# One row in 48 of an output projection's weights loaded in four small transfers, and an announced empty loop at the end of VectorE's list

## The chip, the core and the metric

The kernel runs on one core of one Trainium2 chip. The metric is the device time of one execution in microseconds (us). Before the change three runs took 186.94, 187.01 and 187.04 us, median 187.01.

## What is computed

One decode step of a transformer block with adaptive layer norm, for two sequences of one token each. Cut to what matters:

```
mod = (silu(c) @ w_mod)            -> sa, ca, ga, sb, cb, gb     # 6 vectors of 640 per sequence
h = layernorm(x) * (1 + ca) + sa
q = h @ wq                         # 640 -> 32 heads of 192
k, v = k_cache, v_cache            # the last 1024 positions of each head
o = softmax(q k^T / sqrt(192)) v   # per sequence and head
x = x + ga * (o @ wo)              # 6144 -> 640
h = layernorm(x) * (1 + cb) + sb
x = x + gb * ((gelu(h @ w_gate) * (h @ w_up)) @ w_down)    # 640 -> 1536 -> 640
```

Everything is bfloat16 in memory. 76.88 MB are read in all, most of it the two caches; wo is 6144 x 640, 7.86 MB.

## The kernel before

The five engines each get a list of operations, written in program order by a small scheduler (`_Sched`): `S.op` puts an operation on an engine's list, `S.dma` a transfer on SyncE's (SP's) list, and `emit` (L133) writes each list out with the semaphore waits that reads and writes of named buffers require. There is no planner: an engine runs its list in order, and a wait at the head of a list holds back all that stands behind it. All transfers are issued by SP, so their order on SP's list is the order in which data comes.

A large SBUF buffer `store` holds all the streamed data: four ring slots of 64 cache rows per partition (24576 B each), and a region of 61440 B per partition behind them that first holds wq, then two more k or v pieces, then wo. The work runs so:

1. GpSimd and VectorE build constants; w_mod, c, x, wq and the first k piece are issued.
2. TensorE (PE) computes the modulation (L468), then q (L491), which is spread to all partitions as `qbc`.
3. Scores: for 8 k tiles in two halves, VectorE multiplies a half tile by q (L529), PE adds up over the 192 dimensions with an identity matrix (L548, in a loop over tiles), VectorE reduces the rest (L562).
4. Softmax for both sequences (L566 to L586).
5. Weighted sum: for each of 2 x 4 v tiles VectorE masks the weights per head (`d_mask`, L590) and PE multiplies (`p_pv`, L602). These are called PV(b,t) here.
6. The result is normalized (L615, L619), gathered per head (L627) and copied to `oc` (L672), on which VectorE runs three 32 x 32 block transposes (L675) to give `oT`: 48 pieces `oT[:, t, :]`, piece t holding the rows 48p + t of the 6144-long vector on partition p.
7. wo: row 48p + t of wo stands on partition p, so each partition reads 48 consecutive rows. They come in four transfers of 16, 16, 12 and 4 rows per partition (wo0 to wo3, L681). PE multiplies them as they land (L706), 4 matmuls per t, one for each of four groups of 160 output columns.
8. Second layer norm, w_gate (wg), w_up (wu) and w_down (wd0, wd1, wd2: 6, 4 and 2 of 12 rows per partition; L747), the residual, and the output transfer.

`warm` (L517) are PE matmuls whose result nobody reads. Two waits on SP's list matter for the change: wo0 to wo3 wait for PV(0,2) and PV(0,3), whose v tiles lay where wo goes (L682); wg and all behind it wait for PV(1,0) and PV(1,1) (L685). Slot 2 of the ring holds the v tile of PV(1,2), slot 3 that of PV(1,3).

Of the kernel before, what the change touches and what calls it, by code (L numbers as in the profile page):

```python
# [1 line left out]

# [2 lines left out]

ALU = mybir.AluOpType
ACTF = mybir.ActivationFunctionType
AX = mybir.AxisListType
BF16 = mybir.dt.bfloat16
F32 = mybir.dt.float32  # L10

_COMPUTE = ("pe", "dve", "act", "pool")

# [58 lines left out]
class _Sched:  # L72
# [57 lines left out]
                need[key] = (d.sem, d.val)  # L130
        return need

    def emit(self, engname, eng, tail=None):  # L133
        waited = {}
        cnt = 0

        def await_all(need):
            for key, (s, v) in need.items():
                if waited.get(key, 0) >= v:
                    continue  # L140
                eng.wait_ge(s, v)
                waited[key] = v

        done = None
        for o in self.lists[engname]:
            if o.loop is not None:
                if o.loop is done:
                    continue
                done = o.loop
                n, ahead, rounds = done.waits(self, engname)  # L150
                await_all(ahead)
                with eng.Fori(0, n) as i:
                    for r in range(done.period):
                        for key, (s, base, step) in rounds[r].items():
                            eng.wait_ge(s, i * step + base)
                        done.body(eng, i, r).then_inc(done.ops[r].sem, 1)
                for r in range(done.period):
                    for key, (s, base, step) in rounds[r].items():
                        waited[key] = max(waited.get(key, 0), base + step * (n - 1))
                cnt += len(done.ops)  # L160
                assert cnt == done.ops[-1].val
                continue
            await_all(self.needs(o, engname))
            last = o.fn(eng)
            if o.inc == 1:
                cnt += 1
                assert cnt == o.val, (engname, o.name, cnt, o.val)
            last.then_inc(o.sem, o.inc)
        if tail is not None:
            tail(eng)  # L170


def bass_adaLN_cond__sliding_block_cached__geglu_ffn__decode_kernel(
# [16 lines left out]
    B, _, D = A_x.shape  # L190
# [4 lines left out]
    SQ = 32  # L195
    NJ = P // SQ
# [4 lines left out]
    DN = D // NJ  # L201
# [9 lines left out]
    NT = NQ // P  # L211
# [3 lines left out]
    NQC = RN // QC  # L215
# [8 lines left out]
    SL = J * Dh  # L224
    WQ_SPLIT = [5]
    assert sum(WQ_SPLIT) == KT
    WO_SPLIT = [16, 16, 12, 4]
    OT_SPLIT = [16, 16, 16]
    assert sum(WO_SPLIT) == NT and sum(OT_SPLIT) == NT
    WU_SPLIT = [5]  # L230
    assert sum(WU_SPLIT) == KT
    WD_SPLIT = [6, 4, 2]
# [8 lines left out]
    with es:  # L241
        S = _Sched(nc, es)
        sb = lambda name, shape, dt: es.enter_context(nc.sbuf_tensor(name, shape, dt))
# [9 lines left out]
        def aux_f(a, n):  # L253
            assert a + n <= NAUX
            return aux[:, a:a + n]
# [8 lines left out]
        def tile_f(slot, n=1):  # L264
            return store[:, slot * SL:(slot + n) * SL]
# [7 lines left out]
        oc = aux_f(0, RN)  # L273
# [4 lines left out]
        ident_b = sb("ident_b", [P, P], BF16)  # L278
        ident_f = sb("ident_f", [P, P], F32)
        one = sb("one", [1, 1], F32)  # L280
        G32 = sb("G32", [P, SQ], F32)
        M32 = sb("M32", [P, H], F32)
        M32b = sb("M32b", [P, H], BF16)
        Bsel = sb("Bsel", [P, P], F32)
        SEL = sb("SEL", [P, 2, HM, P], BF16)
        DS = sb("DS", [P, P], F32)
        xc = sb("xc", [P, DN], BF16)
# [20 lines left out]
        gx = sb("gx", [1, H, QP], F32)  # L308
        nb = sb("nb", [P, 1], F32)
        E_sb = sb("E_sb", [P, 2, KP], BF16)  # L310
        Em = sb("Em", [P, 2, J, H], BF16)
        esum = sb("esum", [P, 2], F32)
        rden = sb("rden", [P, 2], F32)
        On = sb("On", [P, 2, Dh], BF16)
        ps = es.enter_context(nc.psum_tensor("ps", [P, 8, 512], F32))
# [7 lines left out]
        BK_M = 0  # L323
        SC = 256

        def bank(k):
            return ("bank", k)
# [4 lines left out]
        sem_wq = [S.sem("d_wq%d" % i) for i in range(len(WQ_SPLIT))]  # L332
        sem_wo = [S.sem("d_wo%d" % i) for i in range(len(WO_SPLIT))]
        sem_wg = S.sem("d_wg")
        sem_wu = [S.sem("d_wu%d" % i) for i in range(len(WU_SPLIT))]
        sem_wd = [S.sem("d_wd%d" % i) for i in range(len(WD_SPLIT))]
        sem_ring = [S.sem("d_ring%d" % i) for i in range(4)]
# [2 lines left out]
        def k_dma(dst, src):  # L340
            return lambda e: e.dma_start(dst, src)  # L341
# [5 lines left out]
        def dram_rows(v):  # L347
# [9 lines left out]
             reads=[("S", 0, 0, 0), ("S", 0, 0, 1), ("S", 0, 1, 0), ("S", 0, 1, 1)], writes=["ident_f"], name="ident_f")  # L357
        S.op("pool", lambda e: e.tensor_copy(out=ident_b[:, :], in_=ident_f[:, :]),
             reads=["ident_f"], writes=["ident_b"], name="ident_b")
# [3 lines left out]
             reads=["ident_f"], writes=["G32"], name="G32")  # L363
        S.op("dve", lambda e: e.tensor_reduce(out=M32[:, :], in_=ident_f[:, :].rearrange("p (h t) -> p h t", t=QP), axis=AX.X, op=ALU.add),
             reads=["ident_f"], writes=["M32"], name="M32")
# [3 lines left out]
             reads=["G32"], writes=["Bsel"], name="Bsel")  # L369
# [3 lines left out]
             reads=["M32"], writes=["DS"], name="DS")  # L373


        for b in range(2):
            S.op("dve", (lambda b: lambda e: e.tensor_copy(
                out=SEL[:, b, :, BS * b:P:SQ], in_=G32[:, :].rearrange("p (j m) -> p m j", m=HM)))(b),
                reads=["G32"], writes=["SEL"], name="SEL%d" % b)
        for b in range(2):  # L380
            for m in range(HM):
# [3 lines left out]
                    reads=["ident_f"], writes=["Qsel"], name="Qsel%d%d" % (b, m))  # L385
# [7 lines left out]
        keep = {}  # L393
# [14 lines left out]
        def slot_of(*it):  # L408
            return place[it]
# [87 lines left out]
        def move(eng, dst, src, reads, writes, name):  # L497
            if eng == "act":
                S.op("act", lambda e: e.activation(out=dst, in_=src, func=ACTF.Copy), reads=reads, writes=writes, name=name)
            else:  # L500
                S.op("dve", lambda e: e.tensor_copy(out=dst, in_=src), reads=reads, writes=writes, name=name)  # L501
# [15 lines left out]
        def warm(n, bk):  # L517
            def f(e):
                last = None
                for _ in range(n):  # L520
                    last = e.matmul(ps[:, bk, 0:2 * Dh], lhsT=ident_b[:, :], rhs=qbc[:, :, :].rearrange("p b d -> p (b d)"),  # L521
                                    start=True, stop=True)
                return last
            if n:
                S.op("pe", f, reads=["ident_b", "qbc"], writes=[bank(bk)], name="warm")
# [144 lines left out]
        assert keep["kv"] == len(items)  # L670
        for c in range(NQC):
            move(("act", "dve")[c % 2], oc[:, QC * c:QC * (c + 1)], ps[:, BK_H + c, 0:QC], [bank(BK_H + c)], [("oc", c)], "oc%d" % c)  # L672
        t0 = 0
        for i, nt in enumerate(OT_SPLIT):
            S.op("dve", (lambda t0, nt: lambda e: e.transpose(oT[:, t0:t0 + nt, :], oc.rearrange("p (q k) -> p k q", k=NT)[:, t0:t0 + nt, :]))(t0, nt),  # L675
                 reads=[("oc", c) for c in range(NQC)], writes=[("oT", t) for t in range(t0, t0 + nt)], name="oT%d" % i)
            t0 += nt

        wo_src = A_wo.rearrange("(p t) n -> p t n", t=NT)
        wo_of = [(sum(WO_SPLIT[:i]), sum(WO_SPLIT[:i + 1])) for i in range(len(WO_SPLIT))]  # L680
        for i, (ta, tb) in enumerate(wo_of):  # L681
            S.dma("sp", k_dma(wo_v[:, ta:tb, :].rearrange("p t n -> p (t n)"), wo_src[:, ta:tb, :].rearrange("p t n -> p (t n)")),  # L682
                  sem_wo[i], writes=[("wo", i)], deps=[keep["pv", 0, t] for t in (NTL - 2, NTL - 1)], name="ld_wo%d" % i)
        assert slot_of("v", 1, 0) == 0 and slot_of("v", 1, 1) == 1
        r3_dead = [keep["pv", 1, 0], keep["pv", 1, 1]]  # L685
        S.dma("sp", k_dma(wg_v.rearrange("p k n -> p (k n)"), B_w_gate.rearrange("(p k) n -> p (k n)", k=KT)), sem_wg,
              writes=["wg"], deps=r3_dead, name="ld_wg")
# [13 lines left out]
        for i, (ta, tb) in enumerate(wo_of):  # L701
            def f(e, ta=ta, tb=tb):
                last = None
                for t in range(ta, tb):
                    for j in range(NJ):
                        last = e.matmul(ps[SQ * j:SQ * j + SQ, BK_M, 0:DN], lhsT=oT[:, t, :], rhs=wo_v[:, t, DN * j:DN * j + DN],  # L706
                                        start=(t == 0), stop=(t == NT - 1), tile_position=(0, SQ * j), skip_group_check=True)
                return last
            S.op("pe", f, reads=[("wo", i)] + [("oT", t) for t in range(ta, tb)], writes=[bank(BK_M)], name="wo%d" % i)
            warm(WO_WARM[i], 1)  # L710

        S.op("dve", lambda e: e.tensor_tensor(out=lnt[:, 0, :], in0=ps[:, BK_M, 0:DN], in1=modC[:, 2, :], op=ALU.mult),  # L712
             reads=[bank(BK_M), ("modC", 0)], writes=[("lnt", 0)], name="ga_attn")
        S.op("dve", lambda e: e.tensor_tensor(out=X2[:, 0, :], in0=lnt[:, 0, :], in1=X2[:, 0, :], op=ALU.add),
             reads=[("lnt", 0)], writes=[("X2", 0)], name="x1")
# [3 lines left out]
        def ffn_gu(bk, wv, key, name, ka, kb):  # L719
            def f(e):  # L720
# [11 lines left out]
             reads=[bank(BK_G[0])], writes=["gl"], name="gelu")  # L732
        k0 = 0
        for ci, nk in enumerate(WU_SPLIT):
# [4 lines left out]
             reads=[bank(BK_G[1]), "gl"], writes=["aC"], name="geglu")  # L739
        to_contraction(aT[:, :, :], aC[:, :], FT, ["aC"], ["aT"], "aT")  # L740
        f0 = 0
        for ci, nf in enumerate(WD_SPLIT):
            def f(e, f0=f0, nf=nf):
# [11 lines left out]
             reads=[bank(BK_C), ("modC", 1)], writes=[("lnt", 1)], name="gb_y")  # L755
        S.op("dve", lambda e: e.tensor_tensor(out=sc[:, :], in0=lnt[:, 1, :], in1=X2[:, 0, :], op=ALU.add),
             reads=[("lnt", 1), ("X2", 0)], writes=["sc"], name="outC")
# [3 lines left out]
        nc.sync.wait_ge(sem_out, 16)  # L761
        S.emit("pool", nc.gpsimd)
        S.emit("act", nc.scalar)
        S.emit("dve", nc.vector)
        S.emit("pe", nc.tensor)


# [26 lines left out]
```

## Time and profile before

| | |
|---|---|
| runs, median (lowest to highest) | 187.01 us (186.94 to 187.04) |
| profiled execution: its own time | 187.73 us |
| profiled execution: span from first to last instruction | 186.5 us (186.47) |
| PE busy | 117.4 us, 63% |
| VectorE (DVE) busy | 106.6 us, 57% |
| ScalarE (ACT) busy | 13.9 us, 7% |
| GpSimd (POOL) busy | 4.9 us, 3% |
| read from HBM | 76.88 MB, 412 GB/s over the span |
| data queue (q1) | 2916 packets, 96.4% of 16 engines' span |

How to read what the prediction shows. The page cuts the span into 40 slices of 4.66 us; in the DMA row each digit is the busy share of the 16 DMA engines in tenths, and the row below is what they moved. The queue list gives packets, MB and the share of the engines' time. The chain of waits lists start (us), length (us) and what ran; "SPq" is SP issuing a transfer. In the timeline a line is start, length, engine, source line, operation, output<-inputs, count, and in brackets the idle time before and what ended it. "Landing" is when a transfer's last semaphore count arrives. The trace also records each DMA packet (queue, start, duration, size), though not which of the 16 engines moved it.

### The profile page before, as it was taken

To read this page: it belongs to the slowest core of one execution; us is meant where nothing else is said; L and a number is where in the kernel's file an instruction comes from. 1 tells how busy PE (TensorE), PEld (TensorE's weight loads), DVE (VectorE), ACT (ScalarE), POOL (GpSimd) and SP (SyncE) were. 2 spreads that over 40 slices of the span, in tenths; PEclk is the share of its full clock that TensorE was granted. 3 is DMA by queue.
4 is the path that set the end of the run, shared out by engine and by line. 5 is a ranking of instruction groups with operands and counts; after the bars stand their busy time and mean duration, and the time that the engine had idled before them with its cause. 6 is when DMAs were issued, how large, how long until landed. Compare 5 with 4: busy or idle time off the path is not lost.

```text
span 186.5 us, 2487 instructions
## 1 busy us (share of the span) xinstructions
PE 117.4 (63%) x1014; PEld 61.6 (33%) x1014; DVE 106.6 (57%) x114; ACT 13.9 (7%) x24; POOL 4.9 (3%) x12
## 2 busy tenths in 40 slices
PE   0004500860079998898988987329964998359854
PEld 0001200540034443444334443125642665236422
DVE  6801600020584999999999994454919453903431
ACT  2001400022000000000000000110010003200400
POOL 8100000000000000000000000000000000000000
PEclk9999999997557999999999999855998799996999
DMA  7999999899998989999998999999899999999980
GB/s 264 395 462 488 448 435 398 358 499 401 443 464 380 485 371 485 411 432 453 401 474 369 496 401 443 453 401 446 364 438 432 427 423 426 415 421 435 412 346 20
DMA packets 2923, 76.99 MB, mean 413 GB/s; under 512 B 356, under 2 KB 356, under 8 KB 868
## 3 DMA queue, kind: packets, MB, share of 16 engines
q1 hardware_dynamic: 2916, 76.88, 96.4%
q8 instruction: 6, 0.10, 0.2%
q14 instruction: 1, 0.01, 0.0%
HBM read 76.88 MB, written 0.00 MB: 412 GB/s over the span
## 4 chain that ended last, share of the span: by engine, by line
DMA 42%; DVE 36%; PE 17%; SPq 1%; ACT 1%; issue 1%; POOL 1%; DVEq 0%; POOLq 0%
DVE store L529 26%; DMA store<-in_A_k_cache_dram 24%; DMA store<-in_B_w_down_dram 17%; PE ps L602 11%; DVE Sg L562 5%; PE ps L548 4%; DVE Em L590 2%; SPq L341 1%; PE ps L541 1%; ACT E_sb L581 1%; PE ps L583 1%; PE ps L577 1%; DVE On L619 0%; ACT On L615 0%; PE ps L570 0%
## 5 line engine op out<-in xcount | busy, mean ns | idle before, releaser
L529 DVE TENSOR_TENSOR store<-store,qbc 128x6144 bf16<-128x6144 bf16 x16 | 53.5, 3347 | 8.8 <-DMA store<-in_A_k_cache_dram 8.8
L548 PE MATMUL ps<-store,ident_b 128*128 x192 | 46.5, 394 | 6.2 <-DVE store L529 6.2
L548 PEld LDWEIGHTS ps<-store,ident_b 128*128 128x128 bf16 x192 | 19.3, 100 | 31.4 <-issue 14.7
L602 PE MATMUL ps<-store,Em 128*64 128x384 bf16 x256 | 25.0, 364 | 6.6 <-DVE Em L590 6.6
L590 DVE TENSOR_TENSOR Em<-E_sb,M32b 128x2048 bf16<-128x2048 bf16 x8 | 18.1, 2288 | 5.9 <-PE ps L602 5.9
L602 PEld LDWEIGHTS ps<-store,Em 128*64 128x64 bf16 x256 | 15.7, 123 | 15.6 <-DVE Em L590 7.7
L541 PE MATMUL ps<-qbc,ident_b 128*128 128x384 bf16 x64 | 13.6, 338 | 10.9 <-DVE store L529 10.9
L468 PE MATMUL ps<-store,scT 128*32 128x480 bf16 x40 | 4.4, 601 | 15.8 <-DVE scT L425 15.8
L562 DVE TENSOR_REDUCE Sg<-ps 128x32 f32<-128x512 f32 x16 | 10.9, 683 | 5.7 <-PE ps L548 5.7
L491 PE MATMUL ps<-store,hT 128*32 128x384 bf16 x80 | 5.7, 470 | 10.7 <-DMA store<-in_A_wq_dram 10.7
L541 PEld LDWEIGHTS ps<-qbc,ident_b 128*128 128x128 bf16 x64 | 6.3, 100 | 17.0 <-issue 11.6
L501 DVE CAST aux<-ps 128x384 bf16<-128x384 f32 x4 | 2.0, 552 | 16.5 <-PE ps L491 15.6
L521 PE MATMUL ps<-qbc,ident_b 128*128 128x384 bf16 x56 | 11.0, 338 | 0.0
L706 PE MATMUL ps<-store,aux 128*32 128x160 bf16 x192 | 5.1, 269 | 5.2 <-issue 2.1
L491 PEld LDWEIGHTS ps<-store,hT 128*32 128x32 bf16 x80 | 3.2, 136 | 13.7 <-issue 11.6
L468 PEld LDWEIGHTS ps<-store,scT 128*32 128x32 bf16 x40 | 1.2, 132 | 17.3 <-DVE scT L425 15.8
L581 ACT ACTIVATE E_sb<-Sg,nb 128x256 bf16<-128x256 f32 x2 | 1.0, 508 | 78.0 <-DVE nb L580 78.0
L521 PEld LDWEIGHTS ps<-qbc,ident_b 128*128 128x128 bf16 x56 | 5.2, 101 | 3.8 <-issue 1.1
L706 PEld LDWEIGHTS ps<-store,aux 128*32 128x32 bf16 x192 | 4.2, 111 | 6.7 <-issue 4.4
L619 DVE TENSOR_SCALAR On<-ps,rden 32x192 bf16<-32x192 f32 x4 | 1.7, 418 | 7.6 <-ACT On L615 7.6
L712 DVE TENSOR_TENSOR lnt<-ps,modC 128x160 f32<-128x160 f32 x1 | 0.3, 325 | 7.8 <-PE ps L706 7.8
L675 DVE STREAM_TRANSPOSE aux<-aux 128x512 bf16<-128x512 bf16 x3 | 4.1, 1430 | 0.1
(70 smaller groups left out, 57.2 us busy)
## 6 DMA issues: line engine op xcount, KB each, us to landing
store<-in_A_k_cache_dram SPq DMA_DIRECT2D x4, 6144.0 KB, 39.7
store<-in_A_v_cache_dram SPq DMA_DIRECT2D x3, 6144.0 KB, 20.8
store<-in_A_wq_dram SPq DMA_DIRECT2D x1, 7680.0 KB, 30.5
store<-in_A_v_cache_dram SPq DMA_DIRECT2D x2, 3072.0 KB, 15.0
store<-in_A_wo_dram SPq DMA_DIRECT2D x2, 2560.0 KB, 21.3
store<-in_w_mod_dram SPq DMA_DIRECT2D x1, 4800.0 KB, 14.1
store<-in_A_wo_dram SPq DMA_DIRECT2D x1, 1920.0 KB, 28.9
store<-in_B_w_gate_dram SPq DMA_DIRECT2D x1, 1920.0 KB, 24.7
```

The costliest lines, as they stand in the source:

```text
L468: last = e.matmul(ps[SQ * j:SQ * j + SQ, bk, 0:3 * DN].rearrange("p (i n) -> p i n", i=3), lhsT=scT[:, k, :], rhs=wm_v[:, k, 3 * part * D: ...
L491: last = e.matmul(ps[SQ * j:SQ * j + SQ, BK_H + c, 0:QC], lhsT=hT[:, k, :], rhs=wq_v[:, k, RN * j + QC * c:RN * j + QC * (c + 1)], start=( ...
L521: last = e.matmul(ps[:, bk, 0:2 * Dh], lhsT=ident_b[:, :], rhs=qbc[:, :, :].rearrange("p b d -> p (b d)"), start=True, stop=True)
L529: S.op("dve", lambda e: e.tensor_tensor(out=tile_v(ks)[:, hf * JH:(hf + 1) * JH, :], in0=tile_v(ks)[:, hf * JH:(hf + 1) * JH, :], in1=qbc[ ...
L541: last = e.matmul(ps[:, BK_W, 0:2 * Dh], lhsT=ident_b[:, :], rhs=qbc[:, :, :].rearrange("p b d -> p (b d)"), start=True, stop=True)
L548: last = e.matmul(o_ap, lhsT=ident_b[:, :], rhs=tile[:, hf * JH:(hf + 1) * JH, ci * GC:(ci + 1) * GC], start=(ci == 0), stop=(ci == NCH - 1))
L562: S.op("dve", lambda e: e.tensor_reduce(out=S_sb[:, b, a:a + JH], in_=ps[:, hf, 0:JH * GC].rearrange("p (j c) -> p j c", j=JH), axis=AX.X, ...
L581: S.op("act", lambda e: e.activation(out=E_sb[:, b, :], in_=S_sb[:, b, :], func=ACTF.Exp, scale=SCALE, bias=nb[:, 0:1], accum_out=esum[:, ...
L590: S.op("dve", lambda e: e.tensor_tensor(out=Em[:, t % 2, :, :], in0=E_sb[:, b, J * t:J * (t + 1)].unsqueeze(2).broadcast_to([P, J, H]), in ...
L602: last = e.matmul(ps[r:r + 2 * H, BK_O, 0:ON], lhsT=Em[:, t % 2, 2 * jp:2 * jp + 2, :].rearrange("p j c -> p (j c)"), rhs=tile_v(vs)[:, 2 ...
L675: S.op("dve", (lambda t0, nt: lambda e: e.transpose(oT[:, t0:t0 + nt, :], oc.rearrange("p (q k) -> p k q", k=NT)[:, t0:t0 + nt, :]))(t0, n ...
L706: last = e.matmul(ps[SQ * j:SQ * j + SQ, BK_M, 0:DN], lhsT=oT[:, t, :], rhs=wo_v[:, t, DN * j:DN * j + DN], start=(t == 0), stop=(t == NT ...
```

## The change

Row 47 of each partition's 48 rows is no longer part of wo0 to wo3. These 128 rows go, in four transfers of 32 rows x 640, to partitions 0 to 31 of ring slot 2, side by side (`wx`, 32 x 2560). Transfer j takes the rows of the partitions 32j to 32j+31, in an order with a slowest dimension of 4 and a next one of 8 on the source's side. Four more transposes, of 32 x 32, make the matching left side `oX`, and 16 matmuls (4 x 4) over 32 partitions add the product to the same PSUM bank, between wo1's and wo2's. The wx transfers stand on SP's list behind wo1 and wait for PV(1,2), which reads slot 2. wo2 shrinks from 12 to 11 rows per partition and the third transpose from 16 to 15 pieces.

VectorE's list gets an instruction ahead of its first operation that announces a branch as likely taken, and, after its last one, a loop of one round with nothing in it: a register move, a branch, an add, and the announced compare-and-branch, which falls through.

```diff
+@contextmanager
+def hinted_loop(nc, eng, n, hint):
+    head, end = "hinted_loop", "hinted_end"
+    engines = OrderedEngineSet([eng.engine])
+    regs = nc.alloc_registers("hinted_i", engines=engines)
+    nc.regs_mov(regs, 0)
+    nc.br(head, engines=engines)
+    with nc.body(head, valid_engines=engines):
+        yield nc.snap(regs, min_val=0, max_val=n - 1)
+        nc.regs_alu(regs, regs, 1, op=mybir.AluOpType.add)
+        eng.br_lt(regs, n, on_true=head, on_false=end).branch_hint(hint)
+    nc.switch_bb(end)
...
-    def emit(self, engname, eng, tail=None):
+    def emit(self, engname, eng, tail=None, hinted_end=False):
...
+        hint = eng.mark_branch_hint_location() if hinted_end else None
         done = None
         for o in self.lists[engname]:
...
+        if hinted_end:
+            with hinted_loop(self.nc, eng, 1, hint):
+                pass
...
-    WO_SPLIT = [16, 16, 12, 4]
-    OT_SPLIT = [16, 16, 16]
-    assert sum(WO_SPLIT) == NT and sum(OT_SPLIT) == NT
+    NB = NT - 1
+    WO_SPLIT = [16, 16, 11, 4]
+    OT_SPLIT = [16, 16, 15]
+    XQ = 4
+    assert sum(WO_SPLIT) == NB and sum(OT_SPLIT) == NB
...
+        oX = sb("oX", [SQ, NJ * SQ], BF16)
...
+        oX_v = oX[:, :].rearrange("p (j a b) -> p j a b", j=NJ, a=XQ)
...
+        for j in range(NJ):
+            S.op("dve", (lambda j: lambda e: e.transpose(oX_v[:, j, :, :], oc.rearrange("p (b a k) -> p k a b", a=XQ, k=NT)[SQ * j:SQ * (j + 1), NB, :, :]))(j),
+                 reads=[("oc", c) for c in range(NQC)], writes=[("oX", j)], name="oX%d" % j)
...
+            if i == 1:
+                vs = slot_of("v", 1, 2)
+                wx = tile_f(vs)[0:SQ, 0:NJ * D]
+                wx_src = A_wo.rearrange("(j b a t) n -> t j a b n", j=NJ, a=XQ, t=NT)
+                for j in range(NJ):
+                    S.dma("sp", k_dma(wx[:, D * j:D * (j + 1)], wx_src[NB, j]), sem_wx, writes=[("wx", j)], deps=[keep["pv", 1, 2]], name="ld_wx%d" % j)
...
+            def fx(e):
+                last = None
+                for t in range(NJ):
+                    for j in range(NJ):
+                        last = e.matmul(ps[SQ * j:SQ * j + SQ, BK_M, 0:DN], lhsT=oX[:, SQ * t:SQ * (t + 1)],
+                                        rhs=wx[:, D * t + DN * j:D * t + DN * j + DN],
+                                        start=False, stop=False, tile_position=(0, SQ * j), skip_group_check=True)
+                return last
+            if i == 2:
+                S.op("pe", fx, reads=[(x, t) for x in ("wx", "oX") for t in range(NJ)], writes=[bank(BK_M)], name="wx")
...
-        S.emit("dve", nc.vector)
+        S.emit("dve", nc.vector, hinted_end=True)
```

More of the change, by code (lines that the diff above doesn't have):

```diff
@@ L1 @@
-from contextlib import ExitStack
+from contextlib import ExitStack, contextmanager
 import concourse.bass as bass
 from concourse import mybir
+from concourse.bass import OrderedEngineSet
 ALU = mybir.AluOpType
@@ L334, in bass_adaLN_cond__sliding_block_cached__geglu_ffn__decode_kernel @@
         sem_wg = S.sem("d_wg")
+        sem_wx = S.sem("d_wx")
         sem_wu = [S.sem("d_wu%d" % i) for i in range(len(WU_SPLIT))]
@@ L706, in f @@
                         last = e.matmul(ps[SQ * j:SQ * j + SQ, BK_M, 0:DN], lhsT=oT[:, t, :], rhs=wo_v[:, t, DN * j:DN * j + DN],
-                                        start=(t == 0), stop=(t == NT - 1), tile_position=(0, SQ * j), skip_group_check=True)
+                                        start=(t == 0), stop=(t == NB - 1), tile_position=(0, SQ * j), skip_group_check=True)
                 return last
+            def fx(e):
[8 more added lines that the diff above has]
+                S.op("pe", fx, reads=[(x, t) for x in ("wx", "oX") for t in range(NJ)], writes=[bank(BK_M)], name="wx")
             S.op("pe", f, reads=[("wo", i)] + [("oT", t) for t in range(ta, tb)], writes=[bank(BK_M)], name="wo%d" % i)
```

## The prediction

> **What bounds the kernel now.** I read the page's 40 slices first, then its queues, then the chain of work that ended last, then the timeline of the last 40 us. The slices and the queue list, from the page:
>
> ```profile
> DMA  7999999899998989999998999999899999999980
> GB/s 264 395 462 488 448 435 398 358 499 401 443 464 380 485 371 485 411 432 453 401 474 369 496 401 443 453 401 446 364 438 432 427 423 426 415 421 435 412 346 20
> ...
> q1 hardware_dynamic: 2916, 76.88, 96.4%
> q8 instruction: 6, 0.10, 0.2%
> q14 instruction: 1, 0.01, 0.0%
> ```
>
> The DMA engines are 90% busy or more nearly from start to end: the kernel is one stream of loads. Only the next-to-last GB/s slice sags (346), so some engines run dry before others. Seven packets are instruction code, not data. The chain of waits from 140 us on:
>
> ```profile
> 149.67 0.33 SPq L341
> ...
> 151.47 32.13 DMA store<-in_B_w_down_dram
> 183.61 0.04 issue
> 183.65 0.35 PE ps L747 x8
> 184.00 0.02 issue
> 184.03 0.34 DVE lnt L754
> 184.37 0.02 issue
> 184.39 0.32 DVE sc L756
> ```
>
> The last w_down load (wd2) is issued 32 us before it lands; what follows (8 matmuls, two DVE operations, the output) is fixed. So the end is set by the **slowest of the 16 DMA engines** working off its queue.
>
> The trace's packet records give those 16 separately. On one engine a packet starts about 3 ns before the recorded end of the one ahead, and each engine must carry the same list of sizes (8 packets of each load, then a 4-byte count). Following these links assigns every packet. Ends of the last data packet, in us:
>
> ```
> seven that also carried a code packet (its start):
>  183.18 (163.9)  182.65 (147.0)  182.53 (179.1)  182.16 (130.1)  182.14 (39.3)  182.13 (170.7)  181.71 (66.7)
> nine without: 181.19 181.18 180.99 180.93 180.73 180.64 180.55 180.53 180.39
> ```
>
> A 16 KB code packet delays its engine by about 1.5 us (1.04 us itself, 0.5 us on the next packet), the 8 KB one at 66.7 by 1.0 (0.33 and 0.66). The latest engine also lost 1.28 us at 133.7, in the first packet of a v load. The tail lasts from 180.39 to 183.18; the last end becomes the landing 0.43 us later, 183.61.
>
> **The change, part by part.**
>
> *Fewer bytes for all.* Row 47 leaves wo2: 8 packets per engine shrink from 15360 to 14080 B. 15360 B follow each other at 0.573 us, 37.3 ns per KB, so each engine loses 8 x 1.25 KB x 37.3 ns = **0.37 us**.
>
> *More bytes for some.* Each new load has a source whose slowest dimension is 4. Those of c and x have this too (4 x 2 rows); by the trace their data runs on the same four engines, and their counts show four arrivals where others show 16. So the four wx loads, 32 rows of 1280 B each, should run on four engines: 8 packets x 4 = 32 packets each. No packet of 1280 B is in the trace. Bounds per packet: 17 ns (spacing of the 320 B ones) and 99 ns (2560 B). I take 53 ns, on the line through 2560 B (99) and 5120 B (193), because rows of 1280 B lie nearest to the 2560 B ones. 32 x 53 ns is 1.69 us (bounds 0.5 and 3.2), with less than 0.05 for the counts. Net on the four: 1.69 - 0.37 = +1.32 us.
>
> Their ends before are 180.39, 180.93, 181.19 and 181.71; after: 181.7, 182.25, 182.5 and 183.0. The others' last is 183.18 - 0.37 = 182.81. So it hangs on the 181.71: that one carries the 8 KB code packet of 66.7.
>
> [...]
>
> *The announced loop.* The 8 KB packet is the only code on q14 after the start; PE's come in 16 KB on q8. When it starts, VectorE has begun 47 operations, ACT, GpSimd and SP rest in waits: I read it as VectorE's list entering its second stretch of code and fetching the next one. The hint stands first in VectorE's list and names a backward branch at its end, within code already there. I expect the fetch then to disappear or move to the start, where no large load is late for it. Value between 0 (stays) and 1.0 us on that engine; I take 1.0. Then it ends at 182.0, the four end by 182.5, and the last is 182.81: **0.37 us earlier** than 183.18. With the fetch in place the last is 183.0: 0.16 us earlier.
>
> The hint itself costs nothing: VectorE's first operation waits until 1.78 us for GpSimd. Without that cover it would cost a few hundredths (VectorE's recorded semaphore waits take 0.02). The move, branch, add and compare behind VectorE's last operation run from 184.71; PE's own loop shows 0.035 for a move, 0.032 for the add, 0.08 (leaving) to 0.23 (taken) for the compare. 0.4 us at most, under the output's flight, which ends at 186.45.
>
> *Queue order.* Before, SP issues wo0 to wo3 from 138.42 and the rest from 149.67. Now wx waits for PV(1,2), and wo2, wo3, wg, wu and the three wd stand behind it. From the timeline:
>
> ```profile
> 149.75 2.29 DVE L590 TENSOR_TENSOR Em<-E_sb,M32b 128x2048 bf16<-128x2048 bf16 x1 [0.40 <-PE ps L602]
> ...
> 152.09 2.42 PEld L602 LDWEIGHTS ps<-store,Em 128*64 128x64 bf16 x32 [0.23 <-DVE Em L590]
> ...
> 158.75 4.13 DVE L675 STREAM_TRANSPOSE aux<-aux 128x512 bf16<-128x512 bf16 x3
> ```
>
> PV(1,2) ends about 152.1, where the weights of PV(1,3) start. Eleven issues follow: four of 0.55 (x took that), seven of 0.43, ending at 157.3. The wx loads are out by 154.3, and a load's first packet follows its issue by 1 us at the start. The earliest engine ends wo1 at 160.37. Six us of queued wo0 and wo1 cover this: cost 0; without that cover up to 6 us.
>
> *VectorE.* Four transposes of 32 x 32 behind the third oT, each between 0.16 (smallest DVE operation) and 0.35 (transpose of 160 columns): 0.6 to 1.4 us, less 0.09 for the shorter third. They end by 164.2. Nobody needs them until PE's wx, and VectorE itself waits 7.8 us for PE there: cost 0.
>
> *PE.* 16 matmuls more and 4 fewer, behind the 8 warm ones and before wo2. The 64 of wo2 and wo3 take 2.32 us from 168.26, 36 ns each, so +0.43 us, but wx is there early and starts after the warm matmuls at 168.3 or before; wo ends within 0.4 us of the old 170.58. Then wg has ended by 176.2 and PE waits for wu until 179.00, so cost 0. PE's list grows by 24 instructions, so its code packets may start a little earlier, at the same price. The ends of wu shrink like the last ones (178.50 to 178.13; the slowest of the four 177.3 without the fetch), so everything before wd2 also comes 0.37 earlier.
>
> **Sum.** The profiled execution took 187.73 us: span 186.47, 1.26 around it. 187.73 - 0.37 = 187.36. The runs' median is 187.01, 0.72 lower; the same step gives **186.64**.
>
> **Rivals.**
>
> 1. *The four become last* (fetch stays, or the runs without profile lack the 1.28 us at 133.7). For: 181.71 + 1.32 is 183.0; without the loss the old last would be 182.65 and the new 182.5. Against: VectorE's branch lies beyond the fetched code's start. Gain 0.15: 186.86.
>
> 2. *Slower: the wx rows collide.* All 163,840 B go to partitions 0 to 31, which other engines fill at the same time. Before, each load reaches all 128 partitions and 16 engines hold 27 GB/s each (49152 B in 1.816 us); no row shows two engines on one place. If an engine's pace is set where it writes, wx takes up to double: 3.4 us, so 181.19 - 0.37 + 3.4 = 184.2, 1.0 us later, 188.0. It decides from 2.0 + 0.37 = 2.4 us of wx per engine (74 ns a packet; 1.85 us if the fetch stays). A milder form, about 187.4, is likelier than the end value.
> [...] No run here shows a collision yet.
>
> 3. *Slower: code missing at VectorE's end.* If the hint suppresses the next stretch of code and the list's end needs it, it is fetched at 184.7. PE shows the price: a code packet at 163.9, and an unexplained wait of 2.11 us before 166.31. Output covers 1.7 of it: 0.4 to 0.7 late, 187.4 to 187.7.
> [...]
>
> 4. *The loads spread over 16 engines.* Then bytes per engine are as before: 187.05.
>
> **Chances.** Forecast 0.50 (own range 186.45 to 186.75), rival 1 0.20, rival 2 0.20, rival 3 0.06, rival 4 0.04. What a measurement can tell is about 0.2%, 0.37 us, which the forecast just reaches: 0.40 of its 0.50 I count as faster, since no term lets the late engines shed less than 0.37, and a spared code packet can add to it. With 0.04 of rival 1: faster 0.44. Same: 0.10 + 0.16 + 0.03 (mild collision) + 0.04 = 0.33. Slower: 0.17 + 0.06 = 0.23. The range is 186.4 to 187.5: it leaves out the collision's end value and half of rival 3.
>
> **What would show it.** Right: landing of wd2 near 183.2; four engines with 32 packets of 1280 B at 53 ns; no q14 packet in mid-run; wo3, wu and wd2 each 0.3 to 0.4 us earlier. Wrong: 1280 B packets over 74 ns, or engines without wx slowed while it runs; a gap in the DMA row at 160 us (late issue); a VectorE instruction after 186 us.

## The result, and the profile after

The changed kernel takes 187.66 us (median of 13 runs, 187.55 to 188.66); the kernel before, run beside it 13 times, 187.05 us (186.81 to 187.53). The ratio is 1.0039, 95% interval 1.0027 to 1.0052: by the medians 0.6 us slower, where 0.4 us faster was forecast. Three of the 13 runs took 188.4 to 188.7 us, the other ten 187.55 to 187.76. The profiled execution of the changed kernel took 187.76 us, close to its median; the one of the kernel before, from which the prediction was summed, lay 0.7 us above its own.

The page of the changed kernel, slices and queues:

```profile
DMA  7999999799998979899897989989899999999991
GB/s 264 395 448 488 488 435 393 337 499 390 453 485 358 506 337 506 380 464 474 369 506 337 506 369 474 464 380 489 348 422 432 416 445 435 336 394 434 418 380 55
...
q1 hardware_dynamic: 3060, 76.88, 96.8%
q8 instruction: 6, 0.10, 0.2%
```

Two things differ from before. The q14 line is gone: the 8 KB code packet of VectorE's list is no longer fetched in mid-run, and none has come in its place ahead of the first instruction (six of 8192 B stand there in both traces). And the 35th GB/s slice (158.5 to 163.2 us) has fallen from 415 to 336, though the DMA row above it still shows 9: the DMA engines count as busy there, but move less. The next view gives a stretch of time, its length, the busy time of PE, its weight loads, VectorE, ScalarE and GpSimd, then the granted clock, the DMA share and GB/s. Before:

```profile
161.00:164.00 3.00, 1.66 (x99) 1.46 (x88) 1.87 (x2) 0.00 (x0) 0.00 (x0) 1.00 1.02 430
```

After:

```profile
157.00:160.00 3.00, 1.21 (x62) 1.04 (x64) 2.90 (x3) 1.42 (x2) 0.00 (x0) 1.00 1.00 422
161.00:164.00 3.00, 0.32 (x12) 0.32 (x16) 1.21 (x5) 0.00 (x0) 0.00 (x0) 0.63 1.00 292
164.00:168.00 4.00, 4.00 (x69) 2.72 (x60) 0.00 (x0) 0.00 (x0) 0.00 (x0) 0.50 1.01 425
```

With the DMA share at 1.00 all through, the rate drops to 292 GB/s for three microseconds and is back at 425 behind them. That is where the wx packets run (160.5 to 163.3 us). Linked into 16 engines as in the prediction, the packets give (in us):

| us | before | after, four engines with wx | after, twelve without |
|---|---|---|---|
| wx, 32 packets of 1280 B | none | 2.30 to 2.45 | none |
| one 1280 B packet, lowest, median, highest | none | 0.055, 0.088, 0.107 | none |
| end of wo1 to end of wo2, no code packet between, wo1 ended by 161.1 | 4.56 to 4.60 | 6.90 to 6.92 | 5.09 to 5.12 |
| a wo2 packet (15360 B before, 14080 B after), quickest | 0.573 | 0.527 | 0.527 |
| last data packet of the latest engine | 183.18 | 183.20 | 183.03 |

With 0.37 us of bytes less, the twelve should show 4.22; they show 5.10. So **engines that carry no wx at all lose 0.88 us** while wx runs: a 14080 B packet that lies in this stretch takes 0.79 us instead of 0.53, one of 20480 B 1.14 instead of 0.77. The chain of waits of the changed kernel (start, length, what):

```profile
150.81 0.71 SPq L366
...
155.03 0.91 SPq L366
...
155.99 2.43 SPq L366
...
158.94 24.71 DMA store<-in_B_w_down_dram
183.64 0.04 issue
183.69 0.35 PE ps L793 x8
184.04 0.02 issue
184.06 0.34 DVE lnt L800
184.40 0.02 issue
184.42 0.33 DVE sc L802
```

The form is the old one: wd2 lands at 183.64 (183.61 before) and the same tail follows. The last issue starts at 158.94 instead of 151.47, but the transfers stay without a gap.

One rule ties the profiles together. The execution's time less the end of its last data packet is 4.55 us before, 4.56 after, and 4.51 to 4.62 in all experiments but one (e7). So the time follows the latest engine.

### The profile page after: what moved, and what is told of

It is laid out like the page before. It is cut to its first block, busy times and chain, and to the rows that moved or that the text cites. A ratio compares the mean times of both kernels' runs of the same rounds, so it can differ in the third digit from the quotient of the medians.

```text
span 186.5 us, 2523 instructions
## 1 busy us (share of the span) xinstructions
PE 117.5 (63%) x1026; PEld 62.1 (33%) x1026; DVE 107.3 (58%) x118; ACT 13.9 (7%) x24; POOL 4.9 (3%) x12
## 4 chain that ended last, share of the span: by engine, by line
DMA 38%; DVE 36%; PE 18%; SPq 5%; issue 1%; ACT 1%; POOL 1%; DVEq 0%; POOLq 0%
DVE store L554 26%; DMA store<-in_A_k_cache_dram 24%; DMA store<-in_B_w_down_dram 13%; PE ps L627 12%; DVE Sg L587 5%; SPq L366 5%; PE ps L573 3%; DVE Em L615 2%; PE ps L566 1%; ACT E_sb L606 1%; PE ps L608 1%; PE ps L602 1%; DVE On L644 0%; ACT On L640 0%; PE ps L595 0%
## 5 line engine op out<-in xcount | busy, mean ns | idle before, releaser
L573 PE MATMUL ps<-store,ident_b 128*128 x192 | 45.2, 386 | 6.2 <-DVE store L554 6.2
L627 PE MATMUL ps<-store,Em 128*64 128x384 bf16 x256 | 24.5, 357 | 6.6 <-DVE Em L615 6.6
L566 PE MATMUL ps<-qbc,ident_b 128*128 128x384 bf16 x64 | 13.6, 338 | 10.5 <-DVE store L554 10.5
L516 PE MATMUL ps<-store,hT 128*32 128x384 bf16 x80 | 6.3, 508 | 10.9 <-DMA store<-in_A_wq_dram 10.9
L546 PE MATMUL ps<-qbc,ident_b 128*128 128x384 bf16 x56 | 11.7, 355 | 0.0
L701 DVE STREAM_TRANSPOSE aux<-aux 128x512 bf16<-128x512 bf16 (+1 forms) x3 | 4.0, 1396 | 0.1
```

The costliest lines, as they stand in the source:

```text
L516: last = e.matmul(ps[SQ * j:SQ * j + SQ, BK_H + c, 0:QC], lhsT=hT[:, k, :], rhs=wq_v[:, k, RN * j + QC * c:RN * j + QC * (c + 1)], start=( ...
L566: last = e.matmul(ps[:, BK_W, 0:2 * Dh], lhsT=ident_b[:, :], rhs=qbc[:, :, :].rearrange("p b d -> p (b d)"), start=True, stop=True)
L573: last = e.matmul(o_ap, lhsT=ident_b[:, :], rhs=tile[:, hf * JH:(hf + 1) * JH, ci * GC:(ci + 1) * GC], start=(ci == 0), stop=(ci == NCH - 1))
L627: last = e.matmul(ps[r:r + 2 * H, BK_O, 0:ON], lhsT=Em[:, t % 2, 2 * jp:2 * jp + 2, :].rearrange("p j c -> p (j c)"), rhs=tile_v(vs)[:, 2 ...
```

## The experiments

The theory formed from the traces, **crossing**: in a load of 128 partitions each engine fills eight partitions of its own (eight packets each, of one partition's bytes; which partitions, no trace tells, so "own", "foreign" and "another's" below are the author's assumption); when an engine writes small packets into partitions that another one fills, all 16 are held up as long as that lasts. Rivals: the source (rows 61,440 B apart in memory), the crowding of 128 rows on 32 partitions, the load on only four engines, and packets that are just dear. Times are medians; ratios are to the kernel before, run on the same chip, and take in all runs. Losses are against 4.22 us from wo1 to wo2, plus an engine's own wx.

| run | 1280 B packet, median | 161 to 164 us, GB/s | wo1 to wo2, engines without wx | last data packet | time, us | ratio, 95% |
|---|---|---|---|---|---|---|
| after | 0.088 | 292 | 5.10 | 183.20 | 187.66 | 1.0039 [1.0027, 1.0052] |
| e1 rows only | 0.086 | 289 | 5.2 to 5.4 | 184.07 | 188.75 | 1.0091 [1.0072, 1.0110] |
| e2 loop only | none | 436 | 4.59 | 182.26 | 186.93 | 0.9996 [0.9986, 1.0005] |
| e3 quadrants | 0.085 | 327 | 4.97 | 183.15 | 187.63 | 1.0041 [1.0022, 1.0059] |
| e4 sixteen | 0.055 | 298 | (all carry wx: 5.6) | 183.60 | 188.29 | 1.0066 [1.0048, 1.0084] |
| e5 consecutive | 0.087 | 296 | 5.1 | 183.21 | 187.80 | 1.0038 [1.0021, 1.0055] |
| e6 own | 0.055 | 431 | 4.22 | 182.53 | 186.89 | 0.9989 [0.9976, 1.0001] |
| e7 own, whole product | 0.055 | 421 | 4.21 | 182.35 | 186.89 | 1.0006 [0.9986, 1.0027] |
| e8 foreign | 0.116 | 223 | 5.81 | 183.72 | 188.57 | 1.0087 [1.0070, 1.0104] |
| e9 eight | 0.055 | 427 | 4.22 | 182.77 | 187.38 | 1.0019 [1.0006, 1.0032] |
| e10 two | 0.078 | 332 | 5.15 to 5.46 | 186.44 | 190.05 | 1.0152 [1.0129, 1.0175] |
| e11 before again | none | 427 | 4.59 | 182.50 | 187.12 | 1 run |

**e1, the rows without the announced loop.**

```diff
-        S.emit("dve", nc.vector, hinted_end=True)
+        S.emit("dve", nc.vector)
```

> The changed kernel without the announced loop; the 128 rows still go to four engines. In the changed kernel's trace the four engines end last (183.20, 183.07, 183.00, 182.90), the 8 KB code packet of 66.7 us is gone, and while the 1280 B packets run, 161.3 to 163.9 us, every engine's packets take about 1.5 times their usual time (14080 B: 0.79 us against 0.53), which costs all of them some 0.88 us. If the loop is what took the code packet away, it comes back here on one engine; if that is one of the four, the end is about 1.0 us later than the changed kernel's, near 188.6; if on another, 187.7. If the loop itself costs the time (rival: code fetched at the list's end), this kernel is as fast as the kernel before, 187.05.

The 1280 B packets of the changed kernel run from 160.5 to 163.3 us, not from 161.3 to 163.9 as said there.

The queue list of e1:

```profile
q1 hardware_dynamic: 3060, 76.88, 96.5%
q8 instruction: 6, 0.10, 0.2%
q14 instruction: 1, 0.01, 0.0%
```

The code packet is back, at 64.7 us, and one of the four engines with wx now ends at 184.07 while the other three end at 182.97 to 183.31. So the announced loop removes the packet, and beside the wx rows that is worth 1.1 us (188.75 against 187.66). Hint and loop are taken out together here; no run has the loop without the hint, so which of the two does it is not shown.

**e2, the announced loop alone.** It is the kernel before, with `hinted_end=True` and what stands behind it.

> The kernel before with the announced loop alone; wo as before. By the runs so far the loop takes away the 8 KB code packet, worth 1.0 us on one engine. That engine is not the last in the kernel before (181.71 against 183.18), so: same as before, 187.0 to 187.1; a gain of some tenths if the engine was the last after all. The profile should lack the first packet's loss of 1.28 us that the profile of before shows at 133.7 us, and then end near 182.6 rather than 183.18.

186.93 us, not to be told from the kernel before. q14 is gone here too, and the loop at the end costs nothing. Taking away the packet's 1.0 us buys nothing here, since its engine was not the latest: in e11, below, it ends at 181.51, the latest at 182.50.

**e3, the 32 rows of transfer j to partitions 32j to 32j+31**, with one transpose and one product over 128 partitions.

```diff
-                wx = tile_f(vs)[0:SQ, 0:NJ * D]
+                wx = tile_f(vs)[:, 0:D]
...
-                    S.dma("sp", k_dma(wx[:, D * j:D * (j + 1)], wx_src[NB, j]), sem_wx, writes=[("wx", j)], deps=[keep["pv", 1, 2]], name="ld_wx%d" % j)
+                    S.dma("sp", k_dma(wx[SQ * j:SQ * (j + 1), :], wx_src[NB, j]), sem_wx, writes=[("wx", j)], deps=[keep["pv", 1, 2]], name="ld_wx%d" % j)
```

> The changed kernel, but transfer j goes to partitions 32j to 32j+31 of 640 columns, so that the 128 rows fill all 128 partitions; the product takes 4 matmuls over 128 partitions in place of 16 over 32. Theory 'crossing' (an engine that writes partitions which another engine fills slows all): each of the four engines still writes 8 partitions side by side per transfer, most of them another's, so the slow-down of about 0.88 us stays, 187.5 to 187.7. Theory 'crowding' (partitions 0 to 31 take more than the others): it goes, and the time is that of the run with own partitions, 186.9.

No better than the change itself. Crowding on 32 partitions falls as the cause.

**e4, sixteen engines with two rows each** in every transfer (`XQ = 32`).

> The changed kernel with a slowest source dimension of 32 in place of 4 (the rows of a transfer in natural order), so that the four transfers should run on 16 engines, two rows each. The same 128 rows, the same partitions 0 to 31. Theory 'place' (rows written to partitions 0 to 31 slow all engines): packets in company still slow, end about 0.5 us or more later than the kernel before. Theory 'few engines' (the loss is the four engines' longer lists, plus what four engines on one kind of row do to the rest): no engine gets more bytes than before, nobody is last by 1.3 us, and the time is that of the kernel before less the code packet, 186.9 to 187.1.

Each engine carries only 8 small packets (0.44 us), yet wo1 to wo2 takes 5.6 us where 4.22 + 0.44 = 4.66 was due. The load on four engines falls too. The 1280 B packets show 55 ns in the median even here (122 at most), though the rate falls to 298 GB/s: their own duration is not a sure sign of the slow-down, the time from wo1 to wo2 is.

**e5, rows that lie next to each other in memory.** wx takes wo's first 128 rows, so other weights than the product needs.

```diff
-                wx_src = A_wo.rearrange("(j b a t) n -> t j a b n", j=NJ, a=XQ, t=NT)
+                wx_src = A_wo[0:P, :].rearrange("(j b a) n -> j a b n", j=NJ, a=XQ)
...
-                    S.dma("sp", k_dma(wx[:, D * j:D * (j + 1)], wx_src[NB, j]), sem_wx, writes=[("wx", j)], deps=[keep["pv", 1, 2]], name="ld_wx%d" % j)
+                    S.dma("sp", k_dma(wx[:, D * j:D * (j + 1)], wx_src[j]), sem_wx, writes=[("wx", j)], deps=[keep["pv", 1, 2]], name="ld_wx%d" % j)
```

> The changed kernel, but the 128 rows are wo's first 128, which stand side by side in memory, in place of every 48th row. It reads other rows of wo than the reference wants. Theory 'source' (rows of 1280 B that lie 60 KB apart make the memory slow for all): the 1280 B packets stay at 55 ns, the others at 0.53 us per 14080 B, and the end comes 0.9 us earlier than the changed kernel's, 186.8. Theory 'place': nothing changes, 187.66.

The packets and the stretch are nearly the same (0.087 us, 296 GB/s), and the time is no shorter: the source falls.

**e6, the same 128 rows in eight transfers of 16, to partitions 0 to 15**, four rows from each engine. The product uses half of them and pairs them with other rows of the vector.

```diff
-                wx = tile_f(vs)[0:SQ, 0:NJ * D]
-                wx_src = A_wo.rearrange("(j b a t) n -> t j a b n", j=NJ, a=XQ, t=NT)
-                for j in range(NJ):
+                wx = tile_f(vs)[0:16, 0:2 * NJ * D]
+                wx_src = A_wo.rearrange("(j b a t) n -> t j a b n", j=2 * NJ, a=XQ, t=NT)
+                for j in range(2 * NJ):
...
```

> [...] Half of the rows are not used in the product, and the others with wrong partners, so the output is not the reference's. Theory 'place' in the form 'two engines write where one can': the slow-down of the other twelve engines goes, end about 0.9 us earlier than the changed kernel's, 186.8. Theory 'source': it stays, 187.66.

The stretch of e6, in the columns explained above:

```profile
161.00:164.00 3.00, 1.00 (x32) 1.00 (x36) 1.87 (x5) 0.00 (x0) 0.00 (x0) 0.82 1.05 431
```

431 GB/s, and the 1280 B packets take 55 ns in the median (68 at most). The engines without wx, and without a code packet between, take 4.20 to 4.26 us from wo1 to wo2: the predicted 0.37 us less than before, with nothing lost.

**e7, e6 with the whole product**: eight transposes and 32 matmuls over 16 partitions, so that all is computed as in the changed kernel.

> Eight transfers of 16 rows to partitions 0 to 15, as in the run with own partitions, with the whole product: eight transposes for oX and 32 matmuls over 16 partitions. Theory 'crossing': 1280 B packets at 55 ns, wo1 to wo2 in 4.2 us on the other engines, end as in the run with own partitions, 186.9, 0.1% faster than before and 0.4% faster than the changed kernel. If the 16 matmuls and 4 transposes more are on the path, up to 0.9 us later.

The packets agree with e6, and so does the median, but the runs fall into two groups: seven took 186.61 to 186.97 us, five 187.62 to 188.31. The profiled execution (187.62 us) is one of the five, and in it PE came last instead of the data; the timeline of e7:

```profile
181.85 0.60 PE L796 MATMUL ps<-store,aux 128*32 128x160 bf16 x24 [0.70 <-DVE aux L452]
...
182.38 0.99 PE L548 MATMUL ps<-qbc,ident_b 128*128 128x384 bf16 x5
...
183.30 0.60 PE L796 MATMUL ps<-store,aux 128*32 128x160 bf16 x24
183.95 0.33 DVE L803 TENSOR_TENSOR lnt<-ps,modC 128x160 f32<-128x160 f32 x1 [2.16 <-PE ps L796]
```

The five warm matmuls between wd0's and wd1's start late and run until 183.3, though the last data packet ended at 182.35. This is the one run whose time isn't the last end + 4.5 us. PE is behind from wo on: it has 16 matmuls more than in e6, and the granted clock stays at 0.50 for longer. From 168 to 172 us e7 shows

```profile
168.00:172.00 4.00, 4.00 (x95) 2.95 (x93) 0.00 (x0) 0.00 (x0) 0.00 (x0) 0.50 1.02 425
```

and e6

```profile
168.00:172.00 4.00, 4.00 (x87) 2.47 (x86) 1.02 (x4) 0.00 (x0) 0.00 (x0) 0.78 1.02 429
```

The 60 matmuls of wo2 and wo3 took 2.19 us in e7 and 1.32 in e6. Whether the other four late runs came about in the same way is not shown, since only one execution was profiled.

**e8, e6 moved to partitions 16 to 31**, still from the four engines that also bring c and x. The product reads old v rows in partitions 0 to 15. The edit is shown against the changed kernel; as in e6 there are eight transfers.

```diff
...
-                    S.dma("sp", k_dma(wx[:, D * j:D * (j + 1)], wx_src[NB, j]), sem_wx, writes=[("wx", j)], deps=[keep["pv", 1, 2]], name="ld_wx%d" % j)
+                    S.dma("sp", k_dma(wx[16:SQ, D * j:D * (j + 1)], wx_src[NB, j]), sem_wx, writes=[("wx", j)], deps=[keep["pv", 1, 2]], name="ld_wx%d" % j)
...
```

> [...] The product reads 32 partitions, half of them old v rows, so the output is not the reference's. Same number of transfers, rows and packets as with partitions 0 to 15. Theory 'crossing': the slow-down is back, 1280 B packets near 90 ns, time 187.5 or more. If it was the smaller transfers that made partitions 0 to 15 fast: 186.9.

The stretch of e8:

```profile
161.00:164.00 3.00, 0.00 (x0) 0.00 (x0) 1.31 (x5) 0.00 (x0) 0.00 (x0) 0.61 1.02 223
```

223 GB/s against e6's 431. Transfers, rows, engines and sizes are those of e6; of the loads only the partitions differ, and that is worth 188.57 - 186.89 = 1.7 us. (PE's wx product, over 32 partitions instead of 16, starts after these loads have landed in both.)

**e9, eight engines with four rows each** (`XQ = 8`): the layout of the change, with one constant different.

> [...] All is computed as in the changed kernel. Crossing: nothing is crossed, so the packets of 1280 B take 55 ns throughout (16 on each of eight engines, 0.88 us), the eight other engines go from wo1 to wo2 in 4.22 us, the eight with wx in 5.1. The last end is 182.3 - 0.37 = 181.9 if no engine with a late code packet is among the eight, and 0.88 later, 182.8, if one is: 186.6 to 187.4. Rival (any burst of small packets from memory to 32 partitions slows all): packets near 90 ns, 5.1 us on engines without wx, 187.7 or more.

The stretch of e9:

```profile
161.00:164.00 3.00, 1.07 (x36) 1.08 (x40) 1.81 (x5) 0.00 (x0) 0.00 (x0) 0.81 1.04 427
```

That nothing is crossed in this layout was the author's assumption, since no trace tells which partitions an engine fills. The run shows 427 GB/s; 128 packets with a median of 55 ns (64 at most); of the eight engines without wx, seven take 4.21 to 4.22 us from wo1 to wo2, and the eighth has a code packet in between. The same 128 rows, to the same 32 partitions in another order, now hold up nobody. Partitions 16 to 31 are written here too, so it is not these partitions as such that made e8 slow. The time is still 187.38 us: the two latest engines (182.77 and 182.44) are among the eight with wx and had carried code packets at 37.7 and 129.9, so 1.5 us of code and 0.86 us of wx add up there.

**e10, two engines with sixteen rows each** (`XQ = 2`).

> The slowest dimension is 2: two engines bring 16 rows of each transfer, 64 packets on each. All is computed as in the changed kernel. Crossing: of the 16 partitions that an engine writes, 12 are filled by others, so packets take more than 55 ns, wx takes 3.5 to 5.8 us on the two, their last end is near 180.8 - 0.37 + 3.5 to 5.8 = 183.9 to 186.2, and the time 188.3 to 190.6. What it tells apart: if each crossing packet holds up all 16 engines, the same number of them (112 of 128, now 96 of 128) costs the engines without wx about as much as before, 0.75 to 0.9 us; if only engines whose partitions are written share with the writer, engines without wx split into two groups, some at 4.22 us from wo1 to wo2 and some later.

How many of the 128 packets cross, here and in the change, no trace shows: 12 of 16, 112 and 96 were the author's estimate. The stretch of e10:

```profile
161.00:164.00 3.00, 1.71 (x104) 1.51 (x96) 2.83 (x6) 0.00 (x0) 0.00 (x0) 1.00 1.01 332
164.00:168.00 4.00, 0.43 (x28) 0.29 (x17) 0.00 (x0) 0.00 (x0) 0.00 (x0) 0.97 0.99 338
```

The rate is lower for as long as wx lasts (4.3 and 4.6 us on the two), and *all* fourteen other engines are late: 5.15 to 5.46 us from wo1 to wo2 where 4.22 was due (6.76 on the one with a code packet of 1.5 us between). There are no two groups, so two writers hold up sixteen engines.

**e11, the kernel before again**, for a second profile.

> The kernel before, for a second profile. If the 1.28 us that one engine lost at 133.7 us in the first profile is particular to that execution, it is gone here, the last data packet ends at 182.2 to 182.7 instead of 183.18, and the profiled execution takes 186.8 to 187.3. If it belongs to the kernel, it is seen again, and an execution of 187.7.

From its chain of waits:

```profile
151.12 31.85 DMA store<-in_B_w_down_dram
182.98 0.04 issue
```

wd2 lands at 182.98 instead of 183.61. No engine loses 1.28 us near 133.7; the last data packet ends at 182.50, and the execution took 187.12 us.

## Why the prediction was wrong

**The step that failed** is the price of "more bytes for some": 32 packets by 53 ns on the four engines, and nothing for the others. 53 ns is right for a 1280 B packet where nothing is held up (55 in e6, e7 and e9). In the change it took 88 in the median: the four needed 2.30 to 2.45 us for wx instead of 1.69, and more behind it, +2.3 us net instead of +1.32. The twelve others, given as 0.37 us earlier, came 0.51 us later (0.88 - 0.37). e6 against e8 (same engines, other partitions: 431 and 223 GB/s), and the change against e9 (same partitions, eight engines instead of four: 292 and 427), show that it goes by which engine writes which partitions, not by the bytes or the rows; nor does the engine count set it (four in e6, in e8 and in the change).

This was rival 2, put at 0.20. Its idea (writes that meet where others fill) agrees with e6, e8 and e9, and its price, 187.4 to 188.0, holds the 187.66; the range's upper end of 187.5 cut most of it off. Its sum had only the four engines with wx pay, and no run or trace from before shows the milder 187.4: it was the author's estimate. The runs showed that all sixteen pay, those without wx 0.51 us net. Which partitions an engine fills, no trace shows; what is measured is that with a slowest dimension of 4 the engines without wx lose 0.88 us, and with one of 8 (e9) nothing. The prediction had asked only on how many engines the rows run, not which partitions each of these writes.

**A second step was particular to one execution**: the latest end of 183.18. In e11 and e2, the same stream without the 1.28 us of 133.7 (e2 also without the 8 KB of code), it is 182.50 and 182.26, so 0.37 us off the others brings the four to the front. e7 and e6 measure the forecast without the slow-down: latest ends of 182.35 and 182.53, on engines with wx, and 186.89 us, no change to be told. Rival 1 named this condition. The 0.37 us was read off an execution in which that loss set the end, and carried over, at a fixed step of 0.72 us, to runs that need not have had it. So with the packets as cheap as predicted, the gain would have been eaten by the four engines; the slow-down then added 0.8 us (187.66 against 186.89). That the forecast of 186.64 lies near e7's faster seven runs is no proof of it: e7's profiled execution is not among them.

**Point by point, the rest.**

- Fewer bytes for all, 0.37 us an engine: right (4.59 to 4.22 in e6, e7, e9). The sum mixes KB of 1000 and of 1024 bytes; with one of them throughout it gives 0.38.
- Four engines with 32 packets each: right.
- The announced loop removes the packet on q14: right; 1.0 us on its engine, 1.1 us of the time in e1. The reason given, that the branch names code already there, was not tested.
- Queue order at no cost: right, though not as told. The timeline of the changed kernel:

```profile
150.72 2.44 PEld L627 LDWEIGHTS ps<-store,Em 128*64 128x64 bf16 x32 [0.32 <-DVE Em L615]
150.81 3.70 SPq L366 DMA_DIRECT2D store<-in_A_wo_dram  x6
...
157.39 4.04 DVE L701 STREAM_TRANSPOSE aux<-aux 128x512 bf16<-128x512 bf16 x3
...
161.36 0.94 DVE L705 STREAM_TRANSPOSE oX<-aux 32x32 bf16<-32x32 bf16 x4
...
168.61 0.46 PE L749 MATMUL ps<-store,oX 32*32 32x160 bf16 x16
```

  PV(1,2) ended at 150.8 (152.1 expected) and SP began at once. Two issues were held, for 0.91 and 2.43 us, and the last ended at 159.37 instead of 157.3; the queued wo0 and wo1 covered that.
- VectorE: 0.94 us for four transposes (0.6 to 1.4 expected), and 0.09 less for the three others (4.04 against 4.13). PE: 0.46 us for wx (0.43 expected), and wo ended at 170.33 instead of 170.58. Both covered, as told.
- Code missing at VectorE's end (rival 3): nothing of it; e2 with the loop is as quick as before.

**What stays open**: why engines that carry no wx are held up as well. The loss per engine was 0.75 (e3) to 1.59 us (e8, all on 16 partitions at once), with 128 packets of 1280 B in both, so their number alone does not set it. Reads and other sizes were not tried. Open too are which of hint and loop removes the fetch, and why the granted clock in e7 stayed low for so long.

None of these versions beats the kernel before: e6 and e7 avoid the slow-down and end at no change, e9 avoids it and ends 0.2% later.

## What to carry to other kernels

A load by few partitions is more than bytes per engine: which engine writes which partitions can slow the loads beside it. No trace here tells whose partitions are whose, so try another order of the rows, and read the GB/s of the stretch (here one constant, 8 instead of 4: 427 instead of 292). Where the latest of 16 engines sets the end, a term is worth only the distance to the second, and a sum that starts from the latest one needs a second profile to show that it is always late.

## What the runs showed of the hardware

- The 128 packets of 1280 B that the change brings to partitions 0 to 31 by four engines, beside loads of all 128, slowed all 16 DMA engines: 20480 B took 1.14 us instead of 0.77, 14080 B 0.79 instead of 0.53, with the DMA share still at 1.00. A busy share does not show it; GB/s does (292, and 223 in e8, against 430).
- A 1280 B packet took 55 ns in the median where no engine was held up (e6, e7, e9), with its rows 61,440 B apart in memory.
- An announced loop, hint and backward branch together, at the end of VectorE's list took away a fetch of 8 KB of code at 65 us, in all ten kernels that had it; the three without (before, twice, and e1) show it at 64.7 to 66.7 us.
- SP's issue of a transfer, 0.43 us as a rule, was held for 2.43 us in the changed kernel, for 1.68 and 2.65 us in e10 and, on the last issue, for 2.33 us in e9. In e6, e7 and e8, with the same 32 small packets on each of four engines but in eight transfers, none was held. So the number of small packets per engine does not set it; the cause was not tried. It cost nothing here.
